# A new item order and new eviction engines for a hand-scheduled kernel of two spectral and two feed-forward blocks

## The chip, the cores and the metric

The kernel runs on one core of one Trainium2 chip. The metric is the device time of one execution in microseconds, the median of three runs. Beside it stands one profiled execution, whose trace gives every instruction's start and duration on the engines: PE (TensorE matmul), PEld (its weight load), DVE (VectorE), ACT (ScalarE), POOL (GpSimd) and SP (SyncE, which only issues DMAs here).

## The reference

Four blocks run one behind the other on `x` of shape [1, 2048, 448] in bfloat16. A spectral block normalises each token, takes a real 2-D Fourier transform over tokens and features, multiplies by a complex weight, transforms back and adds the input. A feed-forward block normalises, multiplies by `w1` (448 x 1792), takes relu and squares it, multiplies by `w2` (1792 x 448) and adds the input. The second pair uses the same weights as the first.

```python
def _A_ref(x, w_r, w_i):
    X = rfft2(x.astype(float32)) * (w_r + 1j * w_i)
    return irfft2(X, s=(S, D)).astype(bfloat16)

def _B_ref(x, w1, b1, w2, b2):
    h = einsum("bsd,df->bsf", x, w1) + b1
    r = where(h > 0, h, 0)
    return einsum("bsf,fd->bsd", r * r, w2) + b2

x = A_x
x = x + _A_ref(_layernorm(x), A_w_r, A_w_i)
x = x + _B_ref(_layernorm(x), B_w1, B_b1, B_w2, B_b2)
x = x + _A_ref(_layernorm(x), A_w_r, A_w_i)
x = x + _B_ref(_layernorm(x), B_w1, B_b1, B_w2, B_b2)
```

## The kernel before

**Stages.** The 2048 tokens are 16 tiles of 128 tokens (partitions) by 448 features. The Fourier transforms are matmuls with constant matrices.

- *First token stage*, tags A1: per tile, mean and variance, the scaling of the constant matrix by 1/std into a buffer `Fs` (`scaled`, L711/712), five matmuls (`first_A`) and an eviction from PSUM into `XA`. Reversed copies of the input rows are made two tiles at a time (tags XR.0 to XR.14, an `evac` of SBUF into SBUF).
- *Spectral stage* (`spectral`), for eight items 1, 2, ..., 7, 0: TD (feature transform, `XA` to `U`), B (second half of the token transform, `U` to `EF`), W (complex products with the weight on DVE, `tensor_tensor` at L729, `EF` through `tmp` to `Z`), Bi (back, `Z` to `VT`). Items p-1 and p share one W, named here by its first item: the chains W.1, W.2, W.4, W.6 and W.0. A tag such as B0.3 or W1.2 carries 0 for the first spectral stage and 1 for the second. TD and B of the larger items fill two PSUM banks and are evicted 896 wide; the smaller ones, 448 wide.
- *Ramp into a feed-forward stage* (`ffn`): for groups of one or two tiles TI and AI (back over features, then the residual add, a `scalar_tensor_tensor` on DVE at L1104), `ln_B` or `ln_rows` (statistics; from tile 4 on `affine` normalised rows, L721 on ACT or L722 on DVE, and a DMA transpose on SP), and for the first tiles `flip`, a transpose on PE with the matrix `J_sb`.
- *Feed-forward*: `h_part` for the first 512 tokens and `h_pairs` for the other three quarters (448 to 1792, relu on ACT, the square on DVE), `o_tile` (1792 to 448, plus the input, DVE at L1245). In the first one each finished tile goes on at once to `second_A`, the token stage of the second spectral block (tags A2); in the second one the output DMAs follow on SP.

**What sets the order.** Every operation is recorded by a helper (`mm`, `act`, `evac`, `scaled`, `affine`, `tt`, `ts`, `cp`, `memset`, `dma`) into a *unit* of `_Sched`, numbered in the order of the program. `ORDER` is a hand-kept dictionary with one list of unit numbers for each engine, and `schedule()` replays these lists: each engine takes its units in exactly this order and waits at a unit until what it needs is there. A unit that may run on several engines (evictions, scalings, affine rows; the table `EV`) runs on the engine in whose list it stands. What `schedule()` still decides itself, from the modelled costs of the operations, is which of the eight PSUM banks a matmul group takes, and where PE gets filler matmuls on a matrix of ones (`warm_mm`, L1352): in a modelled gap of 120 ns or more, if PE was busy for less than 0.7 of the last 3413 ns, or early in the kernel. Since an engine takes no unit out of turn, a unit that is late holds all that stand behind it in its list.

**Units that the prediction speaks of.** On POOL: the clearing of `ones` and `W1_sb`'s last block, the iota and the two gathers of weight rows (units 15 and 16), the clearing of the margin of `Z` (unit 18, the memset of 128 x 1024 into `arena`), the copies XR (20 to 26) and the `Fs` scalings. On PE: b1in's small matmul (unit 42, evicted to `b1col`) and `w1_aux` (unit 160), which makes column sums of `W1_sb`; SP writes those into the last block of `W1_sb`, which the feed-forward matmuls read.

Of the kernel before, what the change touches and what calls it, by code (L numbers as in the profile page):

```python
# [124 lines left out]
1384 1389 1394 1399 1410 1404 1407 1413 1416""",  # L125
    "act": """
# [12 lines left out]
1306 1308 1303 1170 1171 1174 1177 1178 1377 1372 1370 1380 1375 1387 1382 1385 1392 1390 1397 1395 1400 1402""",  # L139
    "dve": """  # L140
# [1290 lines left out]
```

## Time and profile before

| | us |
|---|---|
| median of three runs | 269.94 (269.80, 269.94, 269.97) |
| profiled execution, whole | 269.8 |
| its span in the trace | 267.9 |
| first token stage, with loads | 0 to 18.6 |
| first spectral stage | 18.6 to 43.0 |
| ramp | 43.0 to 50.5 |
| first feed-forward stage, with A2 | 50.5 to 142.5 |
| last tiles of A2, filling of the next stage | 142.5 to 149.4 |
| second spectral stage | 149.4 to 168.2 |
| ramp | 168.2 to 175.4 |
| second feed-forward stage | 175.4 to 265.8 |

The borders are read from the trace: where the first matmul of a stage starts, or DVE's first product. The span runs from the first instruction to the last; what lies around it, 1.9 us, is the start and the end of the program. In a row of the timeline the first two numbers are the start and the time from there to the end of the last instruction of the row; "x5" is the number of instructions, and what stands in brackets is the idle time before them and what ended it. In a row of groups the numbers are busy time, mean ns of one, and idle time before. The granted clock is 1.00 throughout.

### The profile page before, as it was taken

Reading aid. Unit: us, or ns where it says so; the run is one execution under the profiler, and the core shown is the slowest. Engines: PE = TensorE matmul, PEld = TensorE weight load, DVE = VectorE, ACT = ScalarE, POOL = GpSimd, SP = SyncE. Lnnn points to the kernel's source line nnn. Section 1 sums busy time; section 2 is a strip of 40 time slices with the busy share of each in tenths; the row PEclk is TensorE's granted clock in tenths of the full one; section 3 lists DMA queues with packets and bytes.
Section 4 is the critical chain, followed back from the end, with each engine's and each line's share of the span. In section 5 each row is a group of like instructions: output and inputs, shape, how many; then the busy total and the mean of one; then the engine's idle time right before and its main releaser. Section 6 shows DMA issues by size and latency. Waiting matters only on the chain.

```text
span 267.9 us, 5691 instructions
## 1 busy us (share of the span) xinstructions
PE 256.9 (96%) x2090; PEld 165.1 (62%) x2090; DVE 203.7 (76%) x724; ACT 175.6 (66%) x393; POOL 14.9 (6%) x31
## 2 busy tenths in 40 slices
PE   8789998999999999999998998899999999999996
PEld 3667587778544555655567766688654675554454
DVE  3978996999999976299997899689995059734442
ACT  5977899987279746784226897899445885040930
POOL 8940000000000000000000000000000000000000
PEclk9999999999999999999999999999999999999999
DMA  7999410022300215000000000001423100023103
GB/s 232 404 291 347 157 40 1 3 40 42 66 10 20 41 22 107 4 0 2 1 0 2 2 0 0 4 14 30 78 60 68 42 0 0 20 39 92 52 0 103
DMA packets 25554, 16.33 MB, mean 61 GB/s; under 512 B 18186, under 2 KB 24566, under 8 KB 25528
## 3 DMA queue, kind: packets, MB, share of 16 engines
q1 hardware_dynamic: 24792, 14.26, 19.7%
q10 hardware_dynamic: 576, 0.92, 0.9%
q0 software_dynamic: 160, 0.81, 0.7%
q8 instruction: 16, 0.26, 0.4%
q14 instruction: 10, 0.08, 0.1%
HBM read 10.46 MB, written 1.84 MB: 46 GB/s over the span
## 4 chain that ended last, share of the span: by engine, by line
PE 76%; DVE 11%; ACT 7%; POOL 2%; issue 2%; DVEq 0%; ACTq 0%; POOLq 0%
PE ps L675 76%; ACT VT L700 4%; DVE tmp L729 4%; DVE arena L729 2%; DVE x_sb L1104 1%; ACT arena L700 1%; POOL Wt L772 1%; DVE x_sb L1245 1%; ACT arena L694 1%; DVE VT L729 1%; ACT XA L700 1%; DVE st L834 1%; POOL VT L701 1%; POOL W_sb L742 1%; ACT VT L1128 0%
## 5 line engine op out<-in xcount | busy, mean ns | idle before, releaser
L675 PE MATMUL ps<-yT,W_sb 64*128 64x512 bf16 (+1 forms) x770 | 90.2, 346 | 0.1
L675 PE MATMUL ps<-W_sb,arena 128*128 128x448 bf16 (+3 forms) x476 | 87.1, 342 | 0.0
L675 PEld LDWEIGHTS ps<-yT,W_sb 64*128 64x128 bf16 (+1 forms) x770 | 56.2, 95 | 30.3 <-ACT arena L694 1.6
L675 PEld LDWEIGHTS ps<-W_sb,arena 128*128 128x128 bf16 x476 | 45.5, 98 | 38.5 <-DVE arena L729 1.6
L729 DVE TENSOR_TENSOR arena<-arena 128x512 bf16<-128x512 bf16 (+1 forms) x140 | 45.2, 365 | 25.3 <-ACT arena L694 24.9
L694 ACT ACTIVATE arena<-ps,b1col 128x512 bf16<-128x512 f32 x84 | 51.7, 692 | 18.1 <-PE ps L675 17.9
L1128 ACT ACTIVATE VT<-x_sb 128x448 bf16<-128x448 bf16 x32 | 18.5, 581 | 22.4 <-DVE x_sb L1104 22.4
L700 ACT ACTIVATE arena<-ps 128x448 bf16<-128x448 f32 (+1 forms) x42 | 26.2, 723 | 6.0 <-PE ps L675 5.9
L1245 DVE SCALAR_TENSOR_TENSOR x_sb<-ps,arena 128x448 bf16<-128x448 f32 (+3 forms) x26 | 14.7, 582 | 12.5 <-PE ps L675 12.2
L694 ACT ACTIVATE mv<-mv,epst 128x1 f32<-128x1 f32 (+1 forms) x41 | 11.7, 296 | 16.9 <-DVE mv L835 10.8
L700 ACT ACTIVATE XA<-ps 128x512 bf16<-128x512 f32 x28 | 15.3, 594 | 6.0 <-PE ps L675 5.9
L694 ACT ACTIVATE arena<-ps 128x256 bf16<-128x256 f32 x56 | 17.8, 400 | 1.3 <-PE ps L675 1.3
L675 PE MATMUL ps<-arena,G_sb 128*128 128x448 bf16 (+1 forms) x84 | 17.0, 335 | 0.4 <-ACT arena L700 0.4
L675 PE MATMUL ps<-H_sb,arena 128*128 128x256 bf16 x128 | 16.2, 273 | 1.2 <-DVE arena L729 0.8
L675 PE MATMUL ps<-yT,VT 64*128 64x512 bf16 x42 | 15.8, 376 | 0.0
L700 ACT ACTIVATE VT<-ps 128x512 bf16<-128x512 f32 (+1 forms) x30 | 14.5, 631 | 1.4 <-PE ps L675 1.4
L729 DVE TENSOR_TENSOR tmp<-arena,Wt 128x896 bf16<-128x896 bf16 x26 | 14.8, 622 | 0.4 <-ACT arena L700 0.4
L675 PEld LDWEIGHTS ps<-H_sb,arena 128*128 128x128 bf16 x128 | 11.9, 98 | 5.1 <-DVE arena L729 3.3
L700 ACT ACTIVATE tmp<-ps 128x896 bf16<-128x896 f32 (+1 forms) x18 | 14.1, 850 | 1.4 <-PE ps L675 1.4
L675 PE MATMUL ps<-TD_sb,XA 112*128 112x112 bf16 (+1 forms) x184 | 13.9, 229 | 1.0 <-ACT XA L700 1.0
L675 PEld LDWEIGHTS ps<-TD_sb,XA 112*128 112x128 bf16 (+1 forms) x184 | 12.3, 98 | 2.8 <-DVE XA L701 1.2
L1104 DVE SCALAR_TENSOR_TENSOR x_sb<-ps,x_sb 128x448 bf16<-128x448 f32 x16 | 9.8, 620 | 4.5 <-PE ps L675 4.5
(89 smaller groups left out, 295.4 us busy)
## 6 DMA issues: line engine op xcount, KB each, us to landing
out_dram<-x_sb SPq DMA_DIRECT2D x15, 112.0 KB, 1.8
W_sb<-in_B_w_dram SPq DMA_DIRECT2D x1, 1568.0 KB, 10.1
W_sb<-in_B_w_dram SPq DMA_DIRECT2D x1, 1344.0 KB, 10.3
xin<-in_A_x_dram ACTq DMA_DIRECT2D x4, 224.0 KB, 4.8
xin<-in_A_x_dram SPq DMA_DIRECT2D x4, 224.0 KB, 4.2
H_sb<-c_H SPq DMA_DIRECT2D x1, 896.0 KB, 9.4
G_sb<-c_G SPq DMA_DIRECT2D x1, 672.0 KB, 7.9
Wt<-in_A_w_i_dram SPq DMA_DIRECT2D x1, 393.8 KB, 7.3
```

The lines of the kernel that those rows point to most:

```text
L675: return sch.add("pe", lambda e: e.matmul(_res(o), lhsT, rhs, start=start, stop=stop, skip_group_check=skip), [lhsT, rhs], [o], cost=cost, ...
L694: sch.add("act", lambda e: e.activation(o, _res(i), func, **kw), rd, [o], cost=c)
L700: op = sch.add(engs[0], lambda e: e.activation(o, _res(i), ACT.Copy) if h[0].eng == "act" else e.tensor_copy(o, _res(i)), [i], [o], cost=c ...
L701: e.tensor_copy(o, _res(i)), [i], [o], cost=c[engs[0]], unit=unit)
L729: sch.add(eng, lambda e: e.tensor_tensor(o, _res(a), b, op), [a, b], [o], cost=_free(o) / rate + 69.0)
L742: sch.add(eng, lambda e: e.memset(o, v), [], [o], cost=_free(o) / 1.92 + 60.0)
L772: sch.add("pool", lambda e: e.indirect_dma_start(o, None, (A_w_r, A_w_i)[i], bass.IndirectOffsetOnAxis(ix[:], 0)), [ix[:]], [o], is_dma=Tr ...
L834: small(lambda e, si=si, xi=xi: e.bn_stats(si, xi), [xi], [si], _free(xi) / 0.96 + 69.0)
L1104: small(lambda e, xx=xx, xi=xi, r=r, i=i: e.scalar_tensor_tensor(out=xx, in0=_res(r), scalar=1.0, in1=xi, op0=ALU.mult, op1=ALU.add, accum ...
L1128: sch.add("act", lambda e, i=i, o=o, x=x: e.activation(o, x, ACT.Square, accum_out=sd[:, i, 1:2]), [x], [o, sd[:, i, 1:2]], cost=560.0)
L1245: small(lambda e: e.scalar_tensor_tensor(out=o, in0=_res(i), scalar=r[0] if r else 1.0, in1=xb[:, t, d0:d1], op0=ALU.mult, op1=ALU.add), [ ...
```

## The change

The five lists of `ORDER` are replaced, and three cost constants of the planner are changed. The operations are the same: PE has 2090 matmuls in both kernels, 25 of them fillers.

```diff
@@ the planner's costs @@
-            c = (nfree(o, i) + (61.0 if isinstance(i, _PsAP) else 112.0)) / 1.2
+            c = (nfree(o, i) + (78.0 if isinstance(i, _PsAP) else 128.0)) / 1.2
...
-            c = {"act": (n + (61.0 if isinstance(i, _PsAP) else 112.0)) / 1.2, "dve": ...
+            c = {"act": (n + (78.0 if isinstance(i, _PsAP) else 128.0)) / 1.2, "dve": ...
...
                     out=xx, in0=_res(r), scalar=1.0, in1=xi, op0=ALU.mult, op1=ALU.add, accum_out=sd[:, t + i, 0:1]),
-                    [r, xi], [xx, sd[:, t + i, 0:1]], 600.0)
+                    [r, xi], [xx, sd[:, t + i, 0:1]], 545.0)
@@ ORDER, pool @@
-12 17 14 15 16 20 13 19 22 21 52 60 76 25 105 68 92 84 141 144 23 115 118 24 157 154 18
+12 18 17 14 16 15 19 20 13 22 52 21 68 102 76 105 84 23 92 25 144 118 115 24 131 26 154
@@ ORDER, pe (its beginning) @@
-53 61 77 103 106 69 93 85 142 145 116 119 132 129 158 155 168 170 192 174 172 184 186 196 194 190 188 206 208 214 232
-210 216 218 212 42 228 234 260 230 264 160 270 246 254 256 262 272 248 266 268 258 278 280 274 276 282 284 303 286 402
+53 61 69 103 77 106 85 93 142 145 119 116 129 132 158 155 168 170 192 172 174 184 186 206 208 196 190 194 188 214 232
+210 216 218 212 228 234 256 230 246 254 264 258 272 260 248 262 268 160 270 266 276 278 280 274 282 284 42 303 402 286
...
@@ ORDER, sp (its beginning) @@
-3 6 4 10 36 8 30 28 41 29 33 32 31 45 34 27 39 37 46 40 44 38 163 35 164 165 166 167 332 355 376 379 378 399 421 442
+3 6 4 10 8 27 29 36 28 31 30 38 34 32 33 46 39 44 35 45 40 37 41 163 164 165 166 167 332 355 376 378 379 399 421 401
...
```

Twenty-seven units change engine:

- the copy XR.14 from ACT to POOL, the eviction to `b1col` from ACT to DVE, and several `Fs` scalings and evictions of the first token stage among POOL, ACT and DVE;
- in the spectral stages the eviction of TD0.2 (two banks) from DVE to ACT, one eviction of B0.0 from ACT to DVE, those of Bi0.5 and Bi1.5 exchanged between ACT and DVE, and the first eviction of TD1.0 from DVE to ACT;
- nine `affine` rows: five from ACT to DVE, four from DVE to ACT.

The rest changes its place within an engine's list:

- POOL: the clearing of `Z` (18) from the last place to the second; the two gathers exchanged; XR.4 (21) from ahead of the first `Fs` scaling (52) to behind it.
- PE: b1in's matmul (42) from behind B0.3 to behind Bi0.7; `w1_aux` (160) from behind Bi0.2 to behind Bi0.3; TD0.3 ahead of B0.2 and B0.1; TI, AI and flips of both ramps permuted (TI0.10 ahead of TI0.0, TI1.6 ahead of the last flips); in the second spectral stage B1.4 ahead of B1.3 and TD1.4 between the two halves of B1.1; some A2 and o tiles exchanged.
- DVE: in the chain W1.2 one product of W1.4 (unit 1962) stands between the two steps that make `T[3]` and the two writes to `z`.
- SP: the loads of `J_sb` and of most of `G_sb` earlier, the load of `w_r` rows that waits for a gather at the tenth place, the load of b1in last; some output DMAs, the second load of `W1u` and some transposes of the second feed-forward stage exchanged.

More of the change, by code (lines that the diff above doesn't have):

```diff
@@ L114 @@
     "pe": """
[10 rows of a table removed]
-1384 1389 1394 1399 1410 1404 1407 1413 1416""",
-    "act": """
[12 rows of a table removed]
-1306 1308 1303 1170 1171 1174 1177 1178 1377 1372 1370 1380 1375 1387 1382 1385 1392 1390 1397 1395 1400 1402""",
-    "dve": """
[25 rows of a table removed]
-1401 1403 1405 1411 1408 1414 1417""",
[10 rows of a table added]
+1384 1389 1394 1399 1407 1410 1404 1413 1416""",
+    "act": """
[12 rows of a table added]
+1303 1153 1170 1171 1174 1157 1177 1370 1372 1377 1380 1382 1375 1385 1387 1392 1390 1397 1395 1400 1402""",
+    "dve": """
[25 rows of a table added]
+1403 1160 1408 1405 1411 1414 1417""",
     "pool": """
-12 17 14 15 16 20 13 19 22 21 52 60 76 25 105 68 92 84 141 144 23 115 118 24 157 154 18""",
+12 18 17 14 16 15 19 20 13 22 52 21 68 102 76 105 84 23 92 25 144 118 115 24 131 26 154""",
     "sp": """
-3 6 4 10 36 8 30 28 41 29 33 32 31 45 34 27 39 37 46 40 44 38 163 35 164 165 166 167 332 355 376 379 378 399 421 442
-401 463 1050 1073 1094 1096 1117 1138 1268 1265 1097 1274 1362 1159 1180 1318 1365 1359 1315 1368 1271 1406 1412 1312
-1409 1321 1415 1418""",
+3 6 4 10 8 27 29 36 28 31 30 38 34 32 33 46 39 44 35 45 40 37 41 163 164 165 166 167 332 355 376 378 379 399 421 401
+442 463 1050 1073 1094 1096 1117 1274 1097 1138 1271 1159 1180 1362 1318 1359 1315 1368 1268 1365 1409 1265 1312 1321
+1406 1412 1415 1418""",
 }
@@ L697, in evac @@
             n = _free(o)
-            c = {"act": (n + (61.0 if isinstance(i, _PsAP) else 112.0)) / 1.2, "dve": n / (0.96 if isinstance(i, _PsAP) else 1.92) + 69.0, "pool": n + 69.0}
+            c = {"act": (n + (78.0 if isinstance(i, _PsAP) else 128.0)) / 1.2, "dve": n / (0.96 if isinstance(i, _PsAP) else 1.92) + 69.0, "pool": n + 69.0}
             h = []
```

90 rows, old and new, of the table ORDER are left out of this document.

## The prediction

> **What bounds the kernel now.** I read the engines' busy time first, then one window for each stage, then the chain of waits, and then the timeline of each engine around the points where the chain changes engine.
>
> ```profile
> PE 256.9 (96%) x2090; PEld 165.1 (62%) x2090; DVE 203.7 (76%) x724; ACT 175.6 (66%) x393; POOL 14.9 (6%) x31
> ...
> core 0: us, PE busy (x) PEld busy (x) DVE busy (x) ACT busy (x) POOL busy (x), PEclk, DMA share, GB/s
> 8.20:18.60 10.40, 9.22 (x80) 7.48 (x81) 9.08 (x39) 9.62 (x25) 7.86 (x16) 1.00 1.08 360
> 18.60:43.00 24.40, 23.86 (x197) 17.42 (x197) 22.43 (x44) 20.66 (x39) 0.00 (x0) 1.00 0.52 163
> 43.00:50.50 7.50, 6.62 (x85) 5.66 (x85) 5.26 (x23) 6.87 (x16) 0.00 (x0) 1.00 0.01 4
> 50.50:142.50 92.00, 91.90 (x708) 56.03 (x709) 80.26 (x338) 57.11 (x138) 0.00 (x0) 1.00 0.12 26
> 142.50:149.40 6.90, 6.19 (x86) 4.69 (x85) 4.25 (x17) 4.74 (x10) 0.00 (x0) 1.00 0.01 2
> 149.40:168.20 18.80, 17.12 (x172) 12.40 (x169) 18.45 (x37) 17.28 (x31) 0.00 (x0) 1.00 0.01 1
> 168.20:175.40 7.20, 6.05 (x76) 5.14 (x76) 4.51 (x21) 6.40 (x16) 0.00 (x0) 1.00 0.01 3
> 175.40:265.80 90.40, 90.11 (x677) 54.15 (x676) 55.79 (x195) 47.94 (x112) 0.00 (x0) 1.00 0.18 43
> ```
>
> Each row is a stage: length, then the busy time of PE, PEld, DVE, ACT and POOL. The two feed-forward stretches (50.50 to 142.50 and 175.40 to 265.80) are 182.4 us long and PE is idle in them for 0.10 + 0.29 us. The 2090 matmuls stay, so no order can take more than 0.4 us out of 68% of the span; it can only open gaps. What can be won lies in the other stages, where PE is idle for 1.18, 0.54, 0.88, 0.71, 1.68 and 1.15 us, in all 6.14 us. In the second spectral stage (149.40 to 168.20) DVE is busy for 18.45 of 18.80 us: DVE bounds it, not PE.
>
> ```profile
> 7.65 0.48 POOL Fs L712
> ...
> 8.27 6.85 PE ps L675 x60
> ...
> 149.47 1.18 DVE tmp L729 x2
> ...
> 175.49 90.04 PE ps L675 x676
> ```
>
> These are steps of the chain that ended last (start, length, what). It says who holds the end at each place: POOL's scaling before the first real matmul, PE through the first token stage, DVE's products in the spectral stage, and PE without a break from 175.49 to the end.
>
> **The change part by part.** The changed order moves 27 pieces of work from one engine to another and permutes the rest. PE has 2090 matmuls before and after, 25 of them fillers, of which one grows from 128 to 256 columns and one from 256 to 512. The three cost constants are used by the planner only, for the choice of PSUM bank and the fillers; no instruction is made longer by them.
>
> *First token stage (8.20 to 18.60).* POOL now clears Z (unit 18) second, ahead of the clearing of W1, the iota and the gathers, where it was POOL's last; one copy of reversed rows, XR.4 (unit 21), goes behind the first scaling.
>
> ```profile
> L742 POOL MEMSET arena<- 128x1024 bf16 x1 | 1.0, 951 | 0.0
> ...
> 6.11 1.55 POOL L701 COPY VT<-xin 128x448 bf16<-128x448 bf16 x3
> ...
> 8.27 0.27 PE L675 MATMUL ps<-Fs,xin 128*128 128x256 bf16 x1 [1.43 <-POOL Fs L712]
> ...
> 13.61 0.27 PE L675 MATMUL ps<-Fs,m 128*128 128x256 bf16 x1
> 13.87 0.27 PE L675 MATMUL ps<-Fs,xin 128*128 128x256 bf16 x1
> ...
> 14.85 0.27 PE L675 MATMUL ps<-Fs,m 128*128 128x256 bf16 x1
> 15.25 0.27 PE L675 MATMUL ps<-Fs,xin 128*128 128x256 bf16 x1
> ...
> 18.62 1.60 PE L675 MATMUL ps<-TD_sb,XA 128*128 128x224 bf16 x15 [1.00 <-ACT XA L700]
> ```
>
> The memset puts 0.95 us ahead of the first scaling and the copy takes 1.55 / 3 = 0.52 us away: the first real matmul comes 0.43 us later, at 8.70. Two gaps pay for it. Matmuls of this form start 0.11 us apart when nothing is late (60 in 6.85 us of the chain, a gap among them; 5 to a tile). From 13.61 to 13.87 is 0.26, a gap of 0.15, and from 14.85 to 15.25 is 0.40, a gap of 0.29; both times the next tile's scaled factor was late. The new deal of the scalings over POOL, ACT and DVE has these two factors ahead of their matmuls, since the scalings before them are spread over one engine more. The gaps make 0.44, so the run of 16 tiles ends where it did, and the spectral stage starts at 18.62 as before. Term: 0, with the bounds -0.44 (the gaps close and the delay is taken in by waits that were there anyway) and +0.43 (neither gap closes).
>
> *First spectral stage (18.60 to 43.00).* The eviction of TD0.2 (128x896) goes from DVE to ACT, one of B0.0 (128x448) from ACT to DVE.
>
> ```profile
> 20.35 1.09 DVE L701 CAST arena<-ps 128x896 bf16<-128x896 f32 x1 [0.53 <-PE ps L675]
> ...
> 21.74 0.69 DVE L729 TENSOR_TENSOR tmp<-arena 128x448 bf16<-128x448 bf16 x2 [0.30 <-ACT arena L700]
> ...
> L700 ACT ACTIVATE arena<-ps 128x896 bf16<-128x896 f32 x16 | 14.1, 987 | 0.8 <-PE ps L675 0.8
> L700 ACT ACTIVATE arena<-ps 128x448 bf16<-128x448 f32 x26 | 13.2, 560 | 5.2 <-PE ps L675 5.1
> ```
>
> DVE gives up 1.09 us and takes some half of that; ACT takes 0.99 and gives up 0.56. DVE's first product at 21.74 waited 0.30 us for an ACT eviction, not for DVE. ACT is 0.43 us fuller before it (0.987 - 0.560), DVE freer by as much. Since the operands of that first product come from the evictions ahead of TD0.2's, it does not see the longer queue of ACT. I take -0.05, with the bounds -0.20 and +0.43. Evictions of Bi0.5 and Bi1.5 change places on ACT and DVE; each engine has as many as before, so 0.
>
> *Ramps into the two feed-forward stages.* The inverse transforms, residual adds and flips of the first tiles are permuted (TI0.10 ahead of TI0.0, TI1.6 ahead of the last flips).
>
> ```profile
> 45.09 1.57 SPq L667 DMA_DIRECT2D W_sb<-in_B_b_dram  x2
> ...
> 48.76 2.55 ACT L700 ACTIVATE tmp<-ps 128x896 bf16<-128x896 f32 x3
> 50.56 1.70 PE L675 MATMUL ps<-yT,W_sb 128*128 128x256 bf16 x14
> ...
> 173.72 1.72 ACT L700 ACTIVATE tmp<-ps 128x896 bf16<-128x896 f32 x2
> 175.26 0.22 PE L675 MATMUL ps<-J_sb,x_sb 128*128 128x128 bf16 x1
> 175.49 1.70 PE L675 MATMUL ps<-yT,W_sb 128*128 128x256 bf16 x14
> ```
>
> In both ramps the first feed-forward matmul starts 0.05 to 0.10 us after the end of a two-bank ACT eviction: 48.76 + 2 x 0.85 = 50.46 against 50.56, and 173.72 + 1.72 = 175.44 against 175.49. It waits for a PSUM bank. In the first ramp the new order has as many ACT evictions ahead of that one: 0, between -0.23 and +0.30 (a small ACT step ahead of it or behind). In the second the bank that comes free is of an earlier eviction, and PE's own last flip at 175.26 then gates: I take -0.10, between -0.17 (from 175.49 to 175.32, one matmul behind the flip) and +0.20. The bias column b1col and the column sums of W1 (b1in's matmul and w1_aux, both later on PE) only have to be in W1's last block when the 13th feed-forward matmul reads it, some 1.3 us after 50.56; the last of SP's writes for it was issued at 46.66 and its place behind the last product on DVE stays. Of the affine rows five go from ACT to DVE and four the other way:
>
> ```profile
> L721 ACT ACTIVATE arena<-x_sb,mv,rstd 128x448 bf16<-128x448 bf16 x8 | 5.9, 762 | 4.0 <-DVE mv L1171 4.0
> L722 DVE TENSOR_SCALAR arena<-x_sb,rstd,mv 128x448 bf16<-128x448 bf16 x16 | 5.9, 391 | 0.3 <-DMA yT<-arena 0.2
> ```
>
> They cost 0.76 us on ACT or 0.39 on DVE, under feed-forward matmuls that keep PE at 99.9%; if this cover were gone, a later transpose would be late by 0.37 us for each row moved to ACT. The transposes and output DMAs reordered on SP lie under the same matmuls, and SP's loads arrive before the stages that read them; a load queued behind the one that waits for a gather is late only if the gather is, and then it is late under the first spectral stage's 23.86 us of matmuls.
>
> *Second spectral stage (149.40 to 168.20).* In W1.2, a product of W1.4 is put between the two adds and the two writes to z.
>
> ```profile
> 154.23 1.16 DVE L729 TENSOR_TENSOR tmp<-tmp 128x896 bf16<-128x896 bf16 x2
> 155.49 1.16 DVE L729 TENSOR_TENSOR arena<-tmp 128x896 bf16<-128x896 bf16 x2
> ...
> L700 ACT ACTIVATE arena<-ps 128x896 bf16<-128x896 f32 x9 | 7.8, 1033 | 0.0
> ```
>
> The adds start every 0.54 us, so a third would have started at 155.31, but the first write starts at 155.49, since it needs the add just before it: 0.18 us of an empty DVE, and this DVE sets the end of the stage. The inserted product fills it: -0.18. TD1.0's first eviction on ACT delays the first product by 0.06. Sum -0.12. Its risk is that the product moved up needs B1.5's eviction, one of nine back-to-back on ACT, with about 0.06 us to spare.
>
> *Between the feed-forward and the second spectral stage.*
>
> ```profile
> 145.32 0.98 PE L1352 MATMUL ps<-ones 128*128 128x512 bf16 x5
> 146.24 1.73 PE L675 MATMUL ps<-TD_sb,XA 112*128 112x112 bf16 x32
> ```
>
> The fillers before 146.24 (0.98 / 5 = 0.20 us each of 512 columns) grow by 256 columns, 0.10 us, about the slack that they had: +0.03. The feed-forward stretches themselves: 0, at the best -0.1, at the worst +0.5 for an order that leaves PE without a bank once (the length of one 448-wide ACT eviction).
>
> **Sum:** 0 - 0.05 + 0 - 0.10 - 0.12 + 0.03 + 0 = -0.24 us. The profiled execution took 269.8 us (a span of 267.9 and 1.9 around it); the sum gives 269.6. The median of the three runs is 269.94, 0.14 above the profiled one, and so I forecast 269.7.
>
> **The rivals.** *Faster (B).* The first token stage's late start is hidden (-0.44), both ramps lose their wait for a bank (-0.23 and -0.17) and the spectral term holds (-0.12): -0.96, or 269.0. For it: in both ramps the end of an eviction stands right before the first matmul. Against it: PE has flips of its own to do until 0.2 us before the second of those matmuls, and a bank that is free earlier does not move them.
>
> *Slower (A).* B1.5's eviction comes after the product that was moved up. The point from which it decides is the 0.06 us above: with one more 128x896 eviction ahead of it on ACT it is late by 1.03 less that slack, DVE stands still for 0.97 us, and the 0.12 that the stage wins is lost too (DVE is idle for only 0.35 us in the whole stage). -0.24 + 0.12 + 0.97 is +0.85: 270.6 from the profiled execution, some 270.7 beside the median. For it: ACT has no idle time between its nine evictions there. Against it: the number of evictions ahead of B1.5's is the same in both orders.
>
> *No effect (C).* Waits only change places, and what is left are the fillers' 512 - 256 and 256 - 128 columns, 0.16 us at 0.20 us for 512: 270.1.
>
> *A slow clock after a longer idle time (D).*
>
> ```profile
> 1.00 4.88 PE L1352 MATMUL ps<-ones 128*128 128x512 bf16 x11 [1.00 <-POOL ones L742]
> ```
>
> The first 11 fillers take 0.44 us each, the later ones 0.20 (the row at 145.32): PE starts at about half rate, and that costs 11 x 0.24 = 2.7 us over the stretch. The idle time before the first real matmul was 1.43 us and becomes 1.86; if PE fell back to that rate for as long, the end would be 272.4. Against it: 1.43 us had no such effect (60 matmuls in 6.85 us from 8.27 on). The Trainium skill, page "TensorE: Matmul & The Clock Gate", section "What's actually happening", says that the gate is set by a free-running window of about 3.4 us and closes after an idle window; by that rule 1.86 us do not suffice, and if it closed all the same the loss would be estimated at half of 3.4, 1.7 us, for 271.4. The slow first 4.88 us agree with the rule in kind; the granted clock of 1.00 in every window above does not show them.
>
> **How the numbers follow.** The forecast has 0.42, B 0.28, A 0.22, C 0.05, D 0.03. The forecast's own range is 269.3 to 270.3 (the bounds of the terms, of which seldom more than one is reached). A measurement of this kernel can tell about 0.2% from no change, which is 269.40 to 270.48; of the forecast's 0.42 about 0.08 lie below that. So faster 0.28 + 0.08 = 0.36, the same 0.34 + 0.05 = 0.39, slower 0.22 + 0.03 = 0.25. The range of 268.8 to 271.0 holds the forecast, C, all of B but its tail and all of A but its tail.
>
> **What would show it.** The first real matmul at 8.7 and the first TD matmul at 18.6; the first W product at 21.7; the first feed-forward matmul within 0.3 us of 50.6; no step of over 0.1 us between W1.2's adds and the next DVE operation, and the last product of the second spectral stage 0.1 us earlier; the second feed-forward stretch starting 0.2 to 0.3 us earlier, at 175.2, and still about 90.4 us long. I am wrong if a feed-forward stretch has more than 0.5 us of idle PE, if the first TD matmul moves by over 0.4 us, or if DVE waits for ACT in the middle of W1.4 and W1.6.

## The result, and the profile after

The changed kernel takes 268.74 us (median of five runs, 268.49 to 268.93); the kernel before takes 269.91 beside it. The ratio is 0.9954, with a 95% interval of 0.9944 to 0.9965: 1.2 us faster. Forecast were 269.7, with a range from 268.8 to 271.0. The profiled execution took 268.93 us, its span is 266.9 against 267.9.

The busy times on the page of the changed kernel, then its windows at the borders that the prediction used (length, then PE, PEld, DVE, ACT, POOL, granted clock, DMA):

```profile
PE 255.6 (96%) x2090; PEld 167.2 (63%) x2090; DVE 202.4 (76%) x725; ACT 176.6 (66%) x392; POOL 15.0 (6%) x31
```

```profile
8.20:18.60 10.40, 8.97 (x81) 7.83 (x82) 9.23 (x41) 9.31 (x25) 7.96 (x17) 1.00 1.05 341
...
43.00:50.50 7.50, 7.12 (x88) 5.69 (x88) 5.63 (x24) 6.88 (x15) 0.00 (x0) 1.00 0.01 4
```

PE still has 2090 matmuls. In the window of the first ramp it is idle for 0.38 us where it was idle for 0.88, but the windows stand at fixed times and the changed kernel is ahead of them: 0.33 us of this one (50.17 to 50.50) already belong to the feed-forward stage. So what the change gave is read from the handovers between the stages. Those that the prediction named stand in the timeline of PE and in the chain of waits (start, length, what):

```profile
8.64 0.27 PE L675 MATMUL ps<-Fs,xin 128*128 128x256 bf16 x1 [2.75 <-POOL Fs L712]
...
18.53 1.69 PE L675 MATMUL ps<-TD_sb,XA 128*128 128x224 bf16 x16 [0.99 <-ACT XA L700]
...
50.17 2.03 PE L675 MATMUL ps<-yT,W_sb 128*128 128x256 bf16 x17
...
174.69 2.04 PE L675 MATMUL ps<-yT,W_sb 128*128 128x256 bf16 x17
```

```profile
89.19 4.48 DMA yT<-arena
...
98.35 43.95 PE ps L675 x342
...
149.12 1.18 DVE tmp L729 x2
...
174.22 90.32 PE ps L675 x685
264.56 0.28 DVE x_sb L1245
```

Read against the rows of before, the time between handovers went like this:

| from, to | before | after | change | forecast |
|---|---|---|---|---|
| start to first TD matmul | 18.62 | 18.53 | -0.09 | 0 |
| to first feed-forward matmul | 50.56 - 18.62 = 31.94 | 50.17 - 18.53 = 31.64 | -0.30 | -0.05 |
| to the first W product of the second spectral stage | 149.47 - 50.56 = 98.91 | 149.12 - 50.17 = 98.95 | +0.04 | +0.03 |
| to the first matmul of the second feed-forward stage | 175.49 - 149.47 = 26.02 | 174.69 - 149.12 = 25.57 | -0.45 | -0.22 |
| to the last DVE operation | 265.55 - 175.49 = 90.06 | 264.56 - 174.69 = 89.87 | -0.19 | 0 |

The sum is -0.99 us where the forecast had -0.24. Two rows deserve a second look: in the third a gain and a loss cancel (the loss is at 89.19 in the chain, a wait for a transpose DMA), and in the last one the prediction saw next to nothing to win.

### The profile page after: what moved, and what is told of

Same layout as the page of the kernel before. It is cut to its first block, busy times and chain, and to the rows that moved or that the text cites. A ratio compares the mean times of both kernels' runs of the same rounds, so it can differ in the third digit from the quotient of the medians.

```text
span 266.9 us, 5682 instructions
## 1 busy us (share of the span) xinstructions
PE 255.6 (96%) x2090; PEld 167.2 (63%) x2090; DVE 202.4 (76%) x725; ACT 176.6 (66%) x392; POOL 15.0 (6%) x31
## 4 chain that ended last, share of the span: by engine, by line
PE 64%; DVE 21%; issue 3%; DMA 2%; ACT 2%; DVEq 0%; ACTq 0%
PE ps L675 64%; DVE tmp L729 9%; DVE arena L729 5%; DMA yT<-arena 2%; DVE x_sb L1104 2%; DVE VT L701 1%; ACT tmp L700 1%; DVE xin L729 1%; PE ps L1352 1%; DVE x_sb L1245 1%; DVE tmp L738 0%; DVE arena L722 0%; ACT VT L1128 0%; DVE st L834 0%; DVE Fs L712 0%
## 5 line engine op out<-in xcount | busy, mean ns | idle before, releaser
L675 PEld LDWEIGHTS ps<-yT,W_sb 64*128 64x128 bf16 (+1 forms) x770 | 58.1, 95 | 28.2 <-ACT arena L694 1.7
L700 ACT ACTIVATE arena<-ps 128x448 bf16<-128x448 f32 (+1 forms) x43 | 27.0, 699 | 5.1 <-PE ps L675 4.9
L694 ACT ACTIVATE arena<-ps 128x256 bf16<-128x256 f32 x56 | 18.6, 406 | 1.7 <-PE ps L675 1.5
```

Of the source, the lines that this page charges most:

```text
L675: return sch.add("pe", lambda e: e.matmul(_res(o), lhsT, rhs, start=start, stop=stop, skip_group_check=skip), [lhsT, rhs], [o], cost=cost, ...
L694: sch.add("act", lambda e: e.activation(o, _res(i), func, **kw), rd, [o], cost=c)
L700: op = sch.add(engs[0], lambda e: e.activation(o, _res(i), ACT.Copy) if h[0].eng == "act" else e.tensor_copy(o, _res(i)), [i], [o], cost=c ...
```

## Experiments

`ORDER` can be split into stages, since at several places the old and the new lists hold the same units up to there. So a kernel can have the new order in some stages and the old in the others.

**Is it the order, or the banks that the planner picks?** The first run has the new order under the old constants.

```diff
 ORDER = (as changed)
-            c = (nfree(o, i) + (78.0 if isinstance(i, _PsAP) else 128.0)) / 1.2
+            c = (nfree(o, i) + (61.0 if isinstance(i, _PsAP) else 112.0)) / 1.2
...
-                    [r, xi], [xx, sd[:, t + i, 0:1]], 545.0)
+                    [r, xi], [xx, sd[:, t + i, 0:1]], 600.0)
```

> The new order with the three old cost constants, so that only bank choice and fillers can differ (two fillers of 128 columns stand elsewhere). If the gain comes from the order (waits between engines, stage by stage), the time is that of the changed kernel, 268.7 within 0.2, and the trace has the same starts of stages. If the gain comes from other PSUM banks or fillers, it goes back towards 269.9.

Measured: 270.1 us, ratio 1.0018 (1.0001 to 1.0035). The whole gain was gone. Its timeline agrees with the changed kernel's up to the second feed-forward stage, which it even reaches 0.2 us earlier, and then loses 1.3 us. PE's timeline and the window from 175 to 200 us in both, this run first, then the changed kernel:

```profile
178.94 0.54 PE L675 MATMUL ps<-tmp,FI_sb 128*128 128x224 bf16 x4 [0.30 <-DVE arena L729]
...
187.89 0.54 PE L675 MATMUL ps<-tmp,FI_sb 128*128 128x224 bf16 x4 [0.63 <-ACT arena L694]
```

```profile
175.00:200.00 25.00, 24.07 (x189) 17.56 (x188) 23.43 (x104) 17.44 (x56) 0.00 (x0) 1.00 0.20 41
```

```profile
178.64 0.55 PE L675 MATMUL ps<-tmp,FI_sb 128*128 128x224 bf16 x4
```

```profile
175.00:200.00 25.00, 25.00 (x197) 18.35 (x197) 24.28 (x106) 17.78 (x56) 0.00 (x0) 1.00 0.20 41
```

These are AI1.4 and AI1.8, groups of two banks; the two waits, 0.30 + 0.63 us, are the whole idle time of this window. In the plan of the run AI1.4 takes a pair of banks of which one is read last by the fifth of six relus in a row on ACT (unit 1198); in the changed kernel its pair is read by the second and third of them (units 1189 and 1183). AI1.8 takes a bank of the group issued right ahead of it (relu unit 1222); in the changed kernel it takes two that are read earlier (1258 and 1237). The profile puts the first wait down to a product on DVE that ended at the same moment; the run after this one decides, since it changes the banks alone. Same order, same engines, another bank: PE waits. The next run keeps the old constants but writes out the changed kernel's bank for each of the 330 matmul groups.

```diff
-                b = pick_banks(w.n, start + sum(op.cost for op in u.ops[:u.ops.index(w.first)]), got)[1]
+                b = BANK[len(placed)]
+                placed.append(w)
```

> The new order under the old cost constants, which took 270.1, with the changed kernel's PSUM bank for every matmul group written out as a table; only two fillers are still placed as under the old constants. If the bank choice is what cost 1.3 us in the second feed-forward stage, the time is that of the changed kernel, 268.7 within 0.2. If the fillers or something else of the constants cost it, it stays at 270.1.

Measured: 268.74 us, ratio 0.9955 (0.9942 to 0.9968), the changed kernel's time. The banks are what the constants do. By themselves, under the old order, the new constants do harm:

```diff
 ORDER = (as before)
-            c = (nfree(o, i) + (61.0 if isinstance(i, _PsAP) else 112.0)) / 1.2
+            c = (nfree(o, i) + (78.0 if isinstance(i, _PsAP) else 128.0)) / 1.2
```

> The old order and the old engines with the three new cost constants: only PSUM banks and fillers can differ from the kernel before. If the bank choice by itself brings the gain, 268.7. If the order brings it and the banks only have to fit, 269.9 within 0.3; a loss of up to 1 us is possible, as with the new order under the old constants, where one two-bank group of the second feed-forward stage got a bank whose last eviction was late.

Measured: 270.59 us, ratio 1.0028 (1.0018 to 1.0038). The loss lies again in the second feed-forward stage, which takes 0.72 us longer (175.47 to 266.25 in the profiled execution); its window there, which had 24.99 us of PE before:

```profile
175.00:200.00 25.00, 24.40 (x197) 18.07 (x195) 22.62 (x101) 17.15 (x53) 0.00 (x0) 1.00 0.20 41
```

**Which stage gives what?** Each of the next kernels is the kernel before, old constants, with the stages named in the new order.

```diff
-first token stage, first spectral stage: old lists
+first token stage, loads, first spectral stage: new lists
```

> The old kernel with the new order of the first token stage, the loads and the first spectral stage only. By the two traces the first inverse transform starts 0.16 us earlier there. If the gains of the stages are local and add up, 269.75 (-0.16) and the rest of the trace shifted by that amount as it was; if the gain hangs on the order as a whole (banks handed on from stage to stage), 269.9 or more, with a new wait in the first ramp.

Measured: 269.31 us. Against the 269.94 beside it that is -0.63 by the medians (the interval of the ratio, 0.9974 to 1.0005, just takes in no change, since two of the twelve executions lay at 271.1), and -0.4 by the spans. The first feed-forward matmul is at 50.17, as in the changed kernel, though the ramp has its old order: the expected 0.16 was too little, and the "ramp's" gain was made before the ramp.

```diff
-ramp into the first and into the second feed-forward stage: old lists
+the same: new lists
```

> The old kernel with the new order of the two ramps only. By the two traces the first ramp gives 0.24 and the second 0.26 us. If the ramps' gain is their own (the wait of the first feed-forward matmul for a bank is gone), 269.4 (-0.5). If the ramps only pass on what earlier evictions of the spectral stages gave, 269.9 within 0.1 and the wait before the first feed-forward matmul is as long as before.

Measured: 270.28 us, ratio 1.0011 (1.0002 to 1.0020). The first feed-forward matmul stayed at 50.55. The ramps' own order gives nothing in the first ramp and 0.16 in the second, and the last stage then lost 0.5; why it did is not shown.

```diff
-"act": ... 279 275 281 285 ... 999 997 995 1003 ...
+"act": ... 279 281 277 285 ... 999 993 997 1003 ...
-"dve": ... 277 283 ... 993 1001 ...
+"dve": ... 275 283 ... 995 1001 ...
```

> The old kernel with one thing from the change: the two halves of Bi0.5, and those of Bi1.5, change places between ACT and DVE (ACT takes the later one, DVE the earlier). The prediction priced this exchange at 0. If the ramps' gains come from ACT's queue of evictions at the end of the spectral stages being shorter, the first feed-forward matmul comes 0.2 to 0.4 us earlier in the first ramp and 0.1 to 0.3 in the second: 269.3 to 269.6. If they come from the start of the kernel (0.09) and the ramps' new order, 269.9 within 0.1.

Measured: 269.95 us, ratio 1.0003 (0.9994 to 1.0012). The exchange of the evictions alone gives nothing; that theory fell.

```diff
-first spectral stage: old lists
+first spectral stage: new lists, and SP's loads
```

> The old kernel with the new order of the first spectral stage alone (SP's loads in the new order with it, the first token stage old). If the earlier Bi evictions on ACT are what brings the first feed-forward matmul forward by 0.3 us (ACT's last eviction ended 0.39 us earlier with the new first part), that matmul starts 31.65 us after the first TD matmul, against 31.94 before, and the time is 269.5 to 269.6. If it is the new start, 31.94 and 269.9.

Measured: 269.65 us, ratio 0.9988 (0.9978 to 0.9997). From the first TD matmul (18.61) to the first feed-forward matmul it is 31.64 us, the 0.30 that the changed kernel gains. ACT's last evictions of the stage, before and in this run:

```profile
41.62 1.77 ACT L700 ACTIVATE VT<-ps 128x512 bf16<-128x512 f32 x4
...
43.53 1.18 PE L675 MATMUL ps<-TI_sb,VT 112*128 112x224 bf16 x14 [0.24 <-ACT VT L700]
```

```profile
41.71 1.37 ACT L700 ACTIVATE VT<-ps 128x512 bf16<-128x512 f32 x3
...
42.96 1.73 PE L675 MATMUL ps<-TI_sb,VT 112*128 112x224 bf16 x21 [0.47 <-DVE b1col L701]
...
50.25 0.94 PE L675 MATMUL ps<-yT,W_sb 128*128 128x256 bf16 x7
```

ACT ended its Bi evictions at 41.62 + 1.77 = 43.39, and TI0.1 waited in its middle for the last of them. In the new order ACT ends at 41.71 + 1.37 = 43.08, and PE runs through TI0.1. The chain of waits has the same step of PE in both, before and in this run:

```profile
43.53 2.12 PE ps L675 x28
```

```profile
43.22 2.12 PE ps L675 x28
```

Before, ACT's evictions into `VT` stand in the chain right ahead of it; in this run DVE's do. The 0.31 arrives whole at the first feed-forward matmul (50.56 to 50.25). Which of this stage's moves brings ACT's evictions forward (the earlier TD and Bi matmuls, `b1col` going to DVE) no run separates.

```diff
-second spectral stage and ramp behind it: old lists
+the same: new lists
```

> The old kernel with the new order of the second spectral stage and the second ramp, old constants. From DVE's first product to the first feed-forward matmul it was 26.02 us before and 25.56 after the change. If these stages' gain is their order's own, 25.56 here; what the last stage then does depends on the banks that it gets (89.2 to 90.5 us from its first matmul to the end in the kernels so far), so 269.5 if they fit and up to 270.6 if not.

Measured: 269.81 us, ratio 0.9997 (0.9988 to 1.0006), and 25.85 us from W's first product to the feed-forward stage, not 25.56. DVE's part of it is 0.20 shorter, as in the changed kernel; the ramp behind it looks as long as before. The whole new order has 25.57 under either set of constants, so that the second ramp gains 0.25 there. The traces say where this goes. A row of PE before, then a step of this run's chain of waits:

```profile
168.98 1.60 PE L675 MATMUL ps<-TI_sb,VT 112*128 112x224 bf16 x15 [0.23 <-ACT VT L700]
```

```profile
173.33 0.32 issue
```

Before, TI waits for ACT's last Bi eviction, as in the first ramp. This wait is gone in the changed kernel and in this run, which brings 0.10. The ramp's own order brings the other 0.15, as the run with the ramps alone shows. This run has both and loses 0.28 again in its profiled execution: behind 173.33 ACT stands still for 0.32 us ahead of a small operation, waiting for nothing that the profile shows, and the last TI group is late by it. Without this pause it would be 25.57. So the gain belongs to these two stages' own order; where the pause comes from stays open.

```diff
 "dve": ... 925 924
-942 927 926 940 943
+927 926 942 940 943
```

> The changed kernel with the inserted product of W1.4 taken back behind the two writes of W1.2. If the insertion gives what the prediction took (0.18 us of empty DVE filled), the second spectral stage ends 0.18 later and the time is 268.9. If the stage's 0.20 comes from the other reordering there (B1.4 ahead of B1.3, W1.6's products), the stage is as long as in the changed kernel and the time 268.7.

Measured: 268.68 us, ratio 0.9968 (0.9952 to 0.9985), too near to the changed kernel to tell by time (two of its twelve executions lay at 270.7). The product is unit 942, not the 1962 that the list of changes names. The trace tells: from W's first product to the first of the last chain it takes 15.72 us, against 15.61 with the product inserted and 15.81 before. The insertion is worth 0.11, the rest of that stage's order 0.09.

**What opened in the first feed-forward stage.** In the changed kernel one affine row of tiles 10 and 11 stands on DVE; it needs a buffer that a transpose DMA still reads, and the queue waits with it. DVE, then PE 4 us later:

```profile
93.77 0.40 DVE L722 TENSOR_SCALAR arena<-x_sb,rstd,mv 128x448 bf16<-128x448 bf16 x1 [0.78 <-DMA yT<-arena]
...
97.46 0.61 PE L675 MATMUL ps<-Fs,tmp 128*128 128x128 bf16 x8
98.34 0.38 PE L675 MATMUL ps<-Fs,tmp 128*128 128x128 bf16 x4 [0.27 <-DVE mv L729]
```

```diff
-"act": ... 418 453      "dve": ... 682 657 419 663 683 658 420
+"act": ... 418 419 453  "dve": ... 682 657 663 683 658 420
```

> The changed kernel with one affine row of tiles 10 and 11 put back from DVE to ACT. In the changed kernel's trace this row stands on DVE for 0.78 us waiting for a transpose DMA, and 4 us later PE waits 0.44 us for a scaling of the second token stage. If the queue behind that wait is what makes PE late, the gap closes and the time falls by 0.3 to 0.44, to 268.3 to 268.4. If PE's gap has another cause (an eviction, a bank), it stays and the time is 268.7.

Measured: 269.01 us, ratio 0.9984 (0.9964 to 1.0004), with five of twelve executions between 270.5 and 270.9. The profiled one is among these, so everything in it comes 1.8 us later. DVE, then PE:

```profile
96.78 0.20 DVE L733 COPY arena<-arena 128x128 bf16<-128x128 bf16 x1 [1.01 <-ACT arena L721]
```

```profile
99.23 0.61 PE L675 MATMUL ps<-Fs,tmp 128*128 128x128 bf16 x8
100.13 0.38 PE L675 MATMUL ps<-Fs,tmp 128*128 128x128 bf16 x4 [0.29 <-DVE mv L1171]
```

The gap stayed at 0.46: the padding copy (unit 420), three places on in DVE's list, now waits for the row on ACT. There it is the second of two affine rows that start at 95.28, right after the transpose has landed (4.2 us after its issue at 90.96). The wait had only changed its place. So the row stays on DVE, and what does not need the transpose goes ahead of it:

```diff
-"dve": ... 682 657 419 663 683 658 420
+"dve": ... 682 657 663 683 658 419 420
```

> The changed kernel with the affine row that waits on DVE for a transpose moved three operations down DVE's list, so that tile 5's additions and statistics and tile 6's scaling run during the wait. If the in-order queue behind that wait is what makes PE stand still for 0.44 us before A2.5, this gap shrinks to below 0.1 and the time falls by 0.35 to 0.44, to about 268.3. If A2.5 is late for another reason, the gap stays and the time is 268.7. (Putting the row on ACT left the gap, since the padding copy behind it on DVE waits for the same transpose.)

Measured: 268.46 us, ratio 0.9956 (0.9943 to 0.9969), nine of ten executions between 268.34 and 268.70 and one at 270.24. DVE and PE there:

```profile
93.01 0.28 DVE L729 TENSOR_TENSOR xin<-x_sb 128x224 bf16<-128x224 bf16 x1
...
93.90 0.38 DVE L722 TENSOR_SCALAR arena<-x_sb,rstd,mv 128x448 bf16<-128x448 bf16 x1
...
97.45 0.83 PE L675 MATMUL ps<-Fs,tmp 128*128 128x128 bf16 x12
98.21 1.03 PE L675 MATMUL ps<-yT,W_sb 64*128 64x512 bf16 x7
```

PE runs through, and the feed-forward matmuls behind start at 98.21 instead of 98.66. Yet this is not 0.45 us in every execution. The run with W1.2's product put back has the changed kernel's order here, and in its profiled execution the transpose came earlier, so that nothing was lost:

```profile
93.17 0.40 DVE L722 TENSOR_SCALAR arena<-x_sb,rstd,mv 128x448 bf16<-128x448 bf16 x1 [0.19 <-DMA yT<-arena]
```

Six profiled executions have this order here. Their DVE waited 0.82, 0.78, 0.54, 0.42, 0.19 and 0 us; the feed-forward matmuls behind started at 98.69, 98.66, 98.42, 98.29, 98.22 and 98.23, and the spans were 266.9, 266.9, 266.7, 266.5, 266.6 and 266.5. So a wait of up to 0.2 costs nothing and a longer one is paid for: this goes most of the way to explain the spread of the changed kernel's times from 268.4 to 268.9. The move lowers the best time little; what it takes away is the long wait.

**The rival of the slow clock.** Three of the first four kernels, those with the new start, had executions 1.8 us above the others. In one of them the profiled execution is such a one. Its PE timeline, fillers first, and two windows with the granted clock (the third number from the end):

```profile
0.99 5.50 PE L1352 MATMUL ps<-ones 128*128 128x512 bf16 x16 [0.99 <-POOL ones L742]
8.64 0.37 PE L675 MATMUL ps<-Fs,xin 128*128 128x256 bf16 x1 [2.16 <-POOL Fs L712]
8.81 0.42 PE L675 MATMUL ps<-Fs,VT 128*128 128x256 bf16 x1
...
11.58 0.42 PE L675 MATMUL ps<-Fs,m 128*128 128x256 bf16 x1
...
11.99 0.27 PE L675 MATMUL ps<-Fs,VT 128*128 128x256 bf16 x1
```

```profile
8.00:10.00 2.00, 1.36 (x7) 1.01 (x8) 2.00 (x12) 1.84 (x7) 1.45 (x4) 0.64 1.02 404
10.00:12.00 2.00, 2.00 (x12) 1.39 (x11) 0.67 (x2) 0.00 (x0) 1.80 (x4) 0.51 1.00 368
```

After 2.16 us of idle time the matmuls start 0.21 us apart where 0.11 is usual, up to 11.79. The trace's record of the granted clock has it full from 5.13 on, half from 8.55 to 11.96, and full again. Half of these 3.41 us is 1.7 us. And the record of each execution gives a mean clock of 0.993 or 0.994 to every execution 1.4 us or more above its fellows, and 0.999 or 1.000 to all others, so that the slow clock is in all of them. The tests of what brings it: fillers in the idle time, and the old start.

```diff
+                if not done_fill:
+                    done_fill = True
+                    for _ in range(8):
+                        self.ops["pe"].append(_Op("pe", self.warm_fn(7, 512), False, 0.0, 195.0))
```

> The changed kernel with eight more fillers of 512 columns ahead of the first real matmul, 8 x 0.2 = 1.6 us at full rate, so that PE is idle for 0.5 to 1.1 us there and not 2.2 to 2.8. If the executions at about +1.8 us (2 to 5 of 12 in three of the last kernels, all with the new start) are PE falling to half rate after that idle time, none of this kernel's executions shows it, and the median is that of the undisturbed ones, 268.7 to 268.9. If they come from elsewhere, they appear at the same rate.

Measured: 268.47 us, ratio 0.9951 (0.9938 to 0.9964), no such execution among five, which at some 2 in 10 would happen by luck one time in three.

```diff
-first token stage, loads: new lists
+first token stage, loads: old lists
```

> The changed kernel (its costs too) with the first token stage and the loads in the old order. The two traces say that the new start gives 0.09 us: 268.8. If the executions at +1.8 us come with the new start's later first matmul, none of 8 or more shows here; without a connection some 2 in 10 do. A loss of up to 1 us is possible if the banks that the planner now hands on fit worse.

Measured: 271.19 us, ratio 1.0051 (1.0036 to 1.0065), and it says nothing on the clock. In the old list of loads the last matrix of `H_sb` stands behind the column sums of `w1_aux`, which the new PE order makes later. PE got it 1.8 us late:

```profile
41.69 1.46 PE L1352 MATMUL ps<-ones 128*128 128x512 bf16 x6
43.48 1.03 PE L675 MATMUL ps<-H_sb,arena 128*128 128x256 bf16 x8 [0.34 <-DMA H_sb<-c_H]
```

So SP's new place for that load is not a detail: with `w1_aux` later on PE, the load has to stand ahead of its writes. The same with the new loads:

```diff
-first token stage: new lists
+first token stage: old lists
```

> The changed kernel with the first token stage in the old order on POOL, ACT, DVE and PE; SP's loads stay in the new order, which the last attempt had put back too, so that the last Bi item waited 1.8 us for its matrix behind the column sums. If the new start is worth only what the trace shows (0.09 us), 268.8, and no execution lies near 270.5; if the first matmul's 0.38 us later start were a real loss, 268.4. If the +1.8 us executions do not come from the start, about 2 in 10 show here.

Measured: 268.39 us, ratio 0.9941 (0.9928 to 0.9955). The new start is worth nothing that can be told in time; what it brings are the late executions.

> The changed kernel once more, unchanged, beside the others of this call: 268.7. If the idle time before its first matmul lets PE fall to half rate in some executions, 1 or 2 in 10 lie at 270.3 to 270.7; in its first five none did.

Measured: 268.57 us, ratio 0.9953 (0.9939 to 0.9967); none of its five executions was late. Over all kernels with the new start and no further fillers 13 of 73 executions lay 1.4 to 2 us above the rest; of 62 with the old start, the run with the late load left out, none. That ties them to the new start. With the eight fillers there were none of ten, which at that rate is luck one time in seven: likely a cure, but not shown. Five of the ten are the next kernel's, which has the moved row too:

> The changed kernel with the affine row moved down DVE's list and with the eight fillers ahead of the first real matmul. If both work as their single runs say, 268.4, with all executions within 0.3 and none near 270.2. If the one execution of ten at +1.8 that the first of them still had comes from elsewhere than PE's idle time at the start, such executions stay.

Measured: 268.50 us, ratio 0.9949 (0.9936 to 0.9962), all executions between 268.46 and 268.56. The last run takes the two weak places away by the moved row and the old start:

> The changed kernel with the first token stage in the old order (the loads in the new one) and with the affine row moved down DVE's list. If the two gaps named (PE's 0.44 us before A2.5 in some executions, and the half rate after the later first matmul in others) are what spreads the changed kernel's times, all executions lie within 0.2 of 268.3. If the time is 268.6 or its executions spread by over 0.4, there is a third cause.

Measured: 268.33 us, ratio 0.9938 (0.9925 to 0.9952), 268.31 to 268.52. That is 1.66 us below the kernel before beside it and 0.2 to 0.4 below the changed kernel's medians (268.57 and 268.74). In five executions no third cause of the spread shows.

## Why the prediction was wrong

The direction was right, the size was a quarter of what came in the profiled execution: -0.24 forecast, -0.99 measured from handover to handover. The time fell below the stated range. The largest step that failed is the forecast of the first spectral stage and its ramp, the next is that of the second pair, and the third is the bound that was set on the feed-forward stages.

- *First spectral stage -0.05 and first ramp 0, since "the new order has as many ACT evictions ahead of that one".* Measured -0.30 together, 0.25 of the 0.75 that were missed, and outside the stage's own bound of -0.20. The prediction followed DVE's first product and then the two-bank eviction at the end of the ramp, for whose bank it let the first feed-forward matmul wait. What set the ramp was its beginning: the end of ACT's Bi evictions, 0.31 us earlier by the order of the spectral stage. The ramp itself is as long as before, and its own order gives nothing. The chain of waits of before has these evictions in it.
- *Second ramp -0.10.* Measured -0.25. The cause given, a bank that comes free earlier, is not what the traces show: 0.10 is TI's wait for ACT's last Bi eviction, which is gone, and 0.15 is the order of the ramp.
- *Second spectral stage -0.12.* Measured -0.20: the mechanism was right, its size was not. The inserted product gives 0.11 (0.18 forecast), the rest of the order 0.09.
- *"No order can take more than 0.4 us out of 68% of the span."* The bound rests on PE's idle time as the windows of busy time give it, 0.10 us in the first feed-forward stage. A matmul of 128 x 256 is recorded for 0.27 us, but the next can start after 0.11; a stall of up to 0.16 leaves PE "busy". The stalls of before stand in its timeline: 7 matmuls that start 0.11 apart take 0.91 where 0.77 would do, 9 take 1.14 for 0.99, and 8 of the second token stage, 0.056 apart, take 0.65 for 0.45. In the second feed-forward stage 7 take 0.84 for 0.77 and 9 take 1.11 for 0.99.

```profile
55.43 0.93 PE L675 MATMUL ps<-yT,W_sb 128*128 128x256 bf16 x7
56.34 0.54 PE L675 MATMUL ps<-tmp,FI_sb 128*128 128x224 bf16 x4
...
65.38 1.15 PE L675 MATMUL ps<-yT,W_sb 128*128 128x256 bf16 x9
66.52 0.54 PE L675 MATMUL ps<-tmp,FI_sb 128*128 128x224 bf16 x4
...
87.23 0.61 PE L675 MATMUL ps<-Fs,tmp 128*128 128x128 bf16 x8
87.88 1.11 PE L675 MATMUL ps<-W_sb,arena 128*128 128x448 bf16 x5
...
180.36 0.93 PE L675 MATMUL ps<-yT,W_sb 128*128 128x256 bf16 x7
181.20 0.57 PE L675 MATMUL ps<-TI_sb,VT 112*128 112x112 bf16 x8
...
188.00 1.15 PE L675 MATMUL ps<-yT,W_sb 128*128 128x256 bf16 x9
189.11 0.54 PE L675 MATMUL ps<-tmp,FI_sb 128*128 128x224 bf16 x4
```

  The first three sum to 0.5 us in a stage that was put at 0.10. The change closes them and opens the 0.44 before A2.5 in some executions, so that in the profiled one +0.04 is left. The last two, 0.2 us, are gone in the changed kernel's trace: this is the -0.19 of the last stage. The Trainium skill, page "Perfetto Trace Analysis", section "Identifying the Most-Contended Engine", says that matmul busy time is a bad measure of the headroom because matmuls are pipelined; these rows agree, the record being longer than the step to the next matmul.
- *"The three cost constants are used by the planner only, for the choice of PSUM bank and the fillers."* True, and then priced at nothing, but for 0.03 of fillers. The banks decide the second feed-forward stage: 0.7 us lost with the new constants and the old order, 1.3 with the old constants and the new order, 0.19 won with both, and the table of banks alone brings 270.1 back to 268.74. Nothing in the first trace gives these numbers, but the bank of each group and its last reader could have been compared in the two plans.
- *First token stage 0.* The first matmul came at 8.64 (8.70 forecast), the two gaps closed, and the stage ended 0.09 earlier. This term was about right.

Of the rivals, B (269.0) came nearest in sum, but not in kind: the waits that went away at the ramps were for ACT's Bi evictions, not for a bank. A did not happen: the stage became shorter. C (270.1) is refuted by the result. D, given 3 in 100, is real: it comes in 13 of 73 executions of the kernels with the new start. Its price was put at 2.7 us from the first fillers and at 1.7 by the page; the run shows 1.8 at the first TD matmul (20.30 against 18.53 in the changed kernel). The forecast gave 0.36 to faster and 0.39 to no change: the error was the confidence that little was to be won.

## What to carry to other kernels

A busy row of a pipelined engine is no proof that there is nothing to win: count the starts of instructions in a stretch and compare them with the closest spacing seen. Where a planner assigns buffers, the assignment is part of the change, even if no instruction moves; compare who last read each buffer before and after. An operation that waits for a DMA belongs behind everything on its queue that does not need it, and idle time ahead of a run of matmuls can cost PE its full clock, 1.7 us here.

## What was unexpected of the hardware

- PE fell to half rate after 2.16 us of idle time. The Trainium skill, page "TensorE: Matmul & The Clock Gate", section "What's actually happening", has a free-running window of about 3.4 us and speaks of at least one idle window. The length agrees: the clock changed at 5.13, 8.55 and 11.96, 3.41 us apart. That the idle time must fill a window does not: here it was shorter.
- The length of the idle time does not decide alone: in the profiled execution of the changed kernel 2.75 us had no effect. The share of a window in which PE works may. From 5.13 to 8.55 PE was busy for 1.35 of 3.41 us, and the clock fell. In the first 3.41 us of full clock PE was busy for 1.47 and 1.49 in the profiled runs of the moved row and of the product put back, and for 1.56 with the old start, whose first matmul comes 0.37 us earlier; there it stayed. That is one slow trace against a few fast ones, so the border is an estimate, and the rule behind it is not shown.
- A transpose DMA of the same size, issued at 89.2 in each of the six executions above, was ready up to 0.8 us earlier or later from one to the next (DVE waited between 0 and 0.82 us for it), and the spans of those executions differ by 0.4.
